# Gated keys transposed by VectorE blocks and DMA instead of TensorE, weights in pieces of 768, first step's layout by products

## Chip, cores and metric

The kernel runs on one core of one Trainium2 chip. The metric is the device time of one execution in microseconds (us), as the median of several runs. On one core a run counts as fast unless it is over 1.5% above the fastest of the same kernel; only fast runs are compared. One run of each kernel is profiled; all views below are of such profiled runs. In them PE is TensorE and PEld its loading of weights, DVE is VectorE, ACT ScalarE, POOL GpSimd and SP SyncE; L486 is line 486 of that kernel's program. PEclk is the clock granted to TensorE, as a share of full speed; in a row of digits each stands for one fortieth of the span, in tenths (9 is 90% or more).

## The reference, cut to what matters

```python
# attention: q, k, v, f_logit are (4, 8, 768, 48)
f = 1.0 / (1.0 + np.exp(-f_logit))
for t in range(S):
    state = f[:, :, t, :, None] * state + np.einsum('bhd,bhe->bhde', k[:, :, t], v[:, :, t])
    y[:, :, t] = np.einsum('bhd,bhde->bhe', q[:, :, t], state)
# bridge: x is (3072, 384); w_in (384, 2048), w_out (2048, 384)
x = y.transpose(0, 2, 1, 3).reshape(B * S, H * D)
h = x @ w_in
g = np.maximum(h, 0.0) + alpha * np.minimum(h, 0.0)
return g @ w_out
```

## The kernel before

The recurrence is computed in chunks of 128 tokens of two batches: 12 **steps** (2 pairs of batches, 6 chunks each). A step has four stages. `prepare` (VectorE and ScalarE) makes products of the gates; `carry` (TensorE) makes `off` (a product of gated queries and keys), transposes the gated keys (`pk`, copied to `ksn`) and computes the update of the state (`pd`, added into `vs`); `attend` makes `raw`, `qu` (masked into `ad`, copied to `A`) and the output `py`, which is copied to `y` and laid out by DMA as `xT`; `network` makes 8 groups of `ph` (each with `neg` on ScalarE and `g` on VectorE) and then 64 `po`. The results of TensorE go to tiles in a memory called PSUM, which the program takes in turn from two pools of banks, as below. In the traces a product that takes a bank again starts after the bank's last reader has ended: `pd` of the kernel before at 80.20 us, 0.10 us after an `ad` (78.25 + 1.85).

```python
psa = ctx.enter_context(tc.tile_pool(name="psa", bufs=2, space=bass.MemoryType.PSUM))
psn = ctx.enter_context(tc.tile_pool(name="psn", bufs=4, space=bass.MemoryType.PSUM))
def pair(name):     # off, pk, pd, raw, qu, py: two pairs of PSUM banks in turn
    return psa.tile([128, 2, 512], F32, tag="pair", name=name)
def bank(name):     # ph, po: four banks in turn
    return psn.tile([128, 512], F32, tag="net", name=name)
# ... in carry:
        pk = pair(f"pk_{i}")
        for u in range(U):
            for hp in range(HP):
                a = (u * HP + hp) * NC2
                nc.tensor.transpose(pk[:, u, hp * 128:(hp + 1) * 128], ks[:, a:a + 2].rearrange("p c s t -> p (c s t)"), ident)
        ksn = work.tile([128, U, HP * 128], F32, tag="ksn", name=f"ksn_{i}", bufs=1)
        for u in range(U):
            nc.scalar.copy(ksn[:, u], pk[:, u])
        yield
        pd = pair(f"pd_{i}")
        # ... 64 small products of ksn and vs
# ... in network:
        for f in range(0, NF, 2):
            ph = bank(f"ph{f}_{i}")
            # ... products of w_in_sb and xT
            nc.scalar.activation(neg, phv, AF.Relu, scale=-1.0)
            for j in range(2):
                nc.vector.scalar_tensor_tensor(g[:, j], neg[:, j], om[:, f + j:f + j + 1], phv[:, j],
                                               ALU.mult, ALU.add)
            yield
        po = [bank(f"po{u}_{i}") for u in range(U)]
        # ... 64 products of g and w_out_sb
```

The weights arrive as 64-bit numbers in pieces of 512 columns. ScalarE makes `pos` and `neg` of a piece, VectorE makes `lead`, `power` and the low part, and an accumulating DMA adds `lead` to it. The instruction order of TensorE, VectorE and ScalarE is set by hand, in strings of letters. `P` is the next part of this step's `prepare`, `Q` the same of the following step, `O` of `carry`, `S` of `attend`, `n` the next group of the previous step's `network`; `a` and `w` are the two halves of a w_in piece, `b` and `v` of a w_out piece; a digit repeats. Each of the three engines is given its instructions in exactly this order.

```python
    first = (
        "P2 a2 P2 w a2 w P O w P a w S2 O w Q S2 a w a S a S Q w2",
        "a P w a w a P w n P a n w b v w S b v n b n O v b v n b v S P S n b O b v n b S v2 n2 S n b v Q b v b n v b v2 Q3 S n Q",
        # ... two more
    )
    usual = "O n2 S n2 S2 n O n Q n Q n S n2 S Q n S Q2 n Q"
```

## Time and profile before

| | before |
|---|---|
| time, median of 3 runs | 657.95 us (657.88 to 659.75) |
| span of the profiled run | 658.4 us |
| TensorE busy | 93% |
| end of step 0 (its last `po`) | 109.97 us |
| a steady step, `off` to `off` | 50.34 us |
| from 10 to 110 us: VectorE busy, DMA share | 92%, 90% |

In a timeline a row has the start, the time from the first to the last of the merged instructions, engine, line, operation, output and inputs; the square bracket says how long the engine sat idle just before, and what ended that. The prediction below shows the main views of the kernel before. Its times for 512, 768 and 1024 elements (684, 954 and 1218 ns) are those of VectorE's TENSOR_TENSOR on fp32 there (`us`, `qd` and `k`).

### The profile page before, as it was taken

To read this page: it belongs to the slowest core of one execution; us is meant where nothing else is said; L and a number is where in the kernel's file an instruction comes from. 1 tells how busy PE (TensorE), PEld (TensorE's weight loads), DVE (VectorE), ACT (ScalarE), POOL (GpSimd) and SP (SyncE) were. 2 spreads that over 40 slices of the span, in tenths; PEclk is the share of its full clock that TensorE was granted. 3 is DMA by queue.
4 is the path that set the end of the run, shared out by engine and by line. 5 is a ranking of instruction groups with operands and counts; after the bars stand their busy time and mean duration, and the time that the engine had idled before them with its cause. 6 is when DMAs were issued, how large, how long until landed. Compare 5 with 4: busy or idle time off the path is not lost.

```text
span 658.4 us, 17032 instructions
## 1 busy us (share of the span) xinstructions
PE 615.5 (93%) x7392; PEld 458.0 (70%) x7392; DVE 420.2 (64%) x897; ACT 267.0 (41%) x493; POOL 69.9 (11%) x109
## 2 busy tenths in 40 slices
PE   0548899999999999999999999999999999999997
PEld 0436766866876876876876876876876786786874
DVE  5999889693863685685585586486387486360220
ACT  5855882543443242451451550550460451431210
POOL 8222332000010000000000001001001000000000
PEclk9857999999999999999999999999999999999999
DMA  6979986122212122112013113023023011001000
GB/s 225 302 207 269 282 233 159 35 65 73 66 37 68 35 52 87 33 40 86 28 53 81 31 62 81 26 66 80 26 66 81 26 34 25 26 2 25 24 1 24
DMA packets 29129, 53.03 MB, mean 81 GB/s; under 512 B 4320, under 2 KB 16864, under 8 KB 29056
## 3 DMA queue, kind: packets, MB, share of 16 engines
q0 software_dynamic: 9616, 27.92, 15.4%
q1 hardware_dynamic: 13584, 21.63, 10.6%
q10 hardware_dynamic: 5856, 2.40, 1.7%
q8 instruction: 58, 0.95, 0.6%
q14 instruction: 15, 0.12, 0.1%
HBM read 36.21 MB, written 4.72 MB: 62 GB/s over the span
## 4 chain that ended last, share of the span: by engine, by line
PE 84%; issue 7%; POOL 4%; DVE 2%; ACT 1%; DMA 1%; POOLq 0%
PE po L502 36%; PE ph L486 35%; PE py L456 3%; PE qu L431 3%; PE raw L416 3%; PE pk L369 2%; PE pd L381 2%; POOL w_in_sb L191 1%; PE off L356 1%; POOL w_out_sb L191 1%; DMA w_out_sb<-w_out_lead 1%; DVE us L289 0%; POOL vs L138 0%; ACT A L340 0%; POOL vs L247 0%
## 5 line engine op out<-in xcount | busy, mean ns | idle before, releaser
L486 PE MATMUL ph<-xT,w_in_sb 128*128 128x256 f32 x1152 | 264.3, 387 | 10.3 <-DMA xT<-y 10.3
L502 PE MATMUL po<-w_out_sb,g 128*128 128x384 f32 x768 | 253.0, 488 | 0.3 <-DMA w_out_sb<-w_out_lead 0.3
L486 PEld LDWEIGHTS ph<-xT,w_in_sb 128*128 128x128 f32 x1152 | 218.1, 192 | 44.7 <-DMA w_in_sb<-w_in_lead 11.3
L502 PEld LDWEIGHTS po<-w_out_sb,g 128*128 128x128 f32 x768 | 144.9, 190 | 97.7 <-DMA w_out_sb<-w_out_lead 0.9
L494 DVE SCALAR_TENSOR_TENSOR g<-neg,om,ph 128x256 f32<-128x256 f32 x192 | 83.1, 476 | 152.0 <-ACT neg L491 151.9
L491 ACT ACTIVATE neg<-ph 128x512 f32<-128x512 f32 x96 | 57.7, 601 | 152.8 <-PE ph L486 124.8
L508 ACT COPY o<-po 128x384 f32<-128x384 f32 x24 | 11.5, 478 | 115.2 <-PE po L502 115.2
L436 DVE COPY_PREDICATED ad<-mquad,qu 128x224 f32<-128x224 int32 (+6 forms) x168 | 50.3, 300 | 8.5 <-DVE ad L422 0.5
L465 ACT COPY y<-py 128x512 f32<-128x512 f32 x24 | 12.9, 591 | 81.2 <-PE py L456 81.2
L289 DVE TENSOR_TENSOR us<-us,fs 128x768 f32<-128x768 f32 (+2 forms) x72 | 44.5, 618 | 0.3
L422 DVE COPY_PREDICATED ad<-mraw,raw 128x256 f32<-128x256 int32 (+1 forms) x96 | 42.3, 441 | 2.7
L445 ACT COPY A<-ad 32x256 f32<-32x256 f32 x96 | 38.4, 400 | 3.8 <-DVE ad L436 2.5
L391 DVE TENSOR_TENSOR vs<-vs,f 48x768 f32<-48x768 f32 x20 | 19.1, 953 | 30.4 <-PE py L456 30.0
L275 ACT COPY us<-qd 128x256 f32<-128x256 f32 x48 | 29.6, 666 | 12.2 <-DVE qd L258 7.4
L258 DVE TENSOR_TENSOR qd<-qd,f 128x768 f32<-128x768 f32 (+2 forms) x36 | 27.1, 752 | 8.2 <-ACT qd L253 8.2
L340 ACT COPY A<-q 48x512 f32<-48x512 f32 x48 | 29.6, 617 | 6.3 <-DMA xT<-y 5.5
L237 POOL DMA_DIRECT2D k<-in_kT x11 | 8.4, 761 | 222.6 <-PE raw L416 197.6
L456 PEld LDWEIGHTS py<-A,vs 128*64 128x64 f32 x768 | 25.1, 145 | 7.2 <-issue 6.2
L431 PE MATMUL qu<-us,k 48*32 48x112 f32 x1536 | 26.4, 265 | 2.6 <-DVE us L289 1.7
L456 PE MATMUL py<-A,vs 128*64 128x64 f32 x768 | 26.9, 231 | 0.9 <-DVE vs L397 0.8
L356 PE MATMUL off<-q,kh 48*32 48x32 f32 x768 | 9.4, 199 | 18.3 <-DVE q L307 18.3
L416 PEld LDWEIGHTS raw<-qd,k 48*32 48x32 f32 x1536 | 18.1, 108 | 10.6 <-issue 10.2
(64 smaller groups left out, 451.1 us busy)
## 6 DMA issues: line engine op xcount, KB each, us to landing
w_in_raw<-in_w_in SPq DMA_DIRECT2D x12, 511.8 KB, 5.9
w_out_raw<-in_w_out SPq DMA_DIRECT2D x12, 511.8 KB, 5.8
f<-in_fT POOLq DMA_DIRECT2D x11, 512.0 KB, 4.1
q<-in_qT POOLq DMA_DIRECT2D x11, 512.0 KB, 4.1
k<-in_kT POOLq DMA_DIRECT2D x11, 512.0 KB, 4.3
out<-o SPq DMA_DIRECT2D x24, 192.0 KB, 1.9
vs<-in_v POOLq DMA_DIRECT2D x22, 192.0 KB, 3.5
w_in_sb<-w_in_lead POOLq DMA_DIRECT2D x12, 256.0 KB, 6.1
```

The costliest lines, as they stand in the source:

```text
L275: nc.scalar.copy(q4[:, :, :, r], qdv[r][:, :, :, 0])
L289: nc.vector.tensor_tensor(us[:, :, UO[m]:UO[m] + 4 * n].rearrange("p g (i r) -> p g i r", r=4), us[:, :, skip:skip + 4 * n].rearrange("p g ...
L416: nc.tensor.matmul(raw[DB * j:DB * (j + 1), par, hp * C:hp * C + QW], lhsT=k[r_, g * DB:(g + 1) * DB], rhs=qd[r_, g], start=True, stop=True)
L422: nc.vector.copy_predicated(adu[:, :, :, d:4], mraw[:, d, :, d:4].bitcast(I32).unsqueeze(1).broadcast_to((128, H, NB, n)), rv[:, :, QO[d]: ...
L431: nc.tensor.matmul(qu[DB * j:DB * (j + 1), par, hp * UW + 4:(hp + 1) * UW], lhsT=k4[r_, g * DB:(g + 1) * DB], rhs=us[r_, g, 4:UW], start=T ...
L436: nc.vector.copy_predicated(ad[:, u, :, :, 4 * m:DB], mquad[:, lo:lo + n].bitcast(I32).unsqueeze(1).unsqueeze(1).broadcast_to((128, 2, HP, ...
L445: nc.scalar.copy(A[s_, u, :, s_], ad[s_, u].rearrange("p r h t -> p (r h) t"))
L456: nc.tensor.matmul(py[64 * par:64 * par + 64, u, o:o + CH], lhsT=vs[bp][:, cc, u, hd * D:hd * D + 64], rhs=A[:, u, par * HP + hp, CH * cc: ...
L486: nc.tensor.matmul(ph[:, j * T:(j + 1) * T], lhsT=w_in_sb[:, kt, (f + j) * 128:(f + j + 1) * 128], rhs=xT[:, kt], start=(kt == 0), stop=(k ...
L491: nc.scalar.activation(neg, phv, AF.Relu, scale=-1.0)
L494: nc.vector.scalar_tensor_tensor(g[:, j], neg[:, j], om[:, f + j:f + j + 1], phv[:, j], ALU.mult, ALU.add)
L502: nc.tensor.matmul(po[u][:, 0:DM], lhsT=gs[f // 2][:, f % 2, u * C:(u + 1) * C], rhs=w_out_sb[:, f], start=(f == 0), stop=(f == NF - 1))
```

## The change

The intent is to take the transposes off TensorE, which is busy nearly all the time, and to shorten the start: fewer and larger weight pieces, and a first layout that needs no DMA. What VectorE's transpose leaves in `kt` is put in place in `ksn` by 16 DMAs a step, 32 rows of `kt` in each. The instruction orders are rewritten as well, that of the start and the usual one. The diff, cut to its core:

```diff
-WP = 512
-RAWS, TOPS, POWERS, LEADS = 5, 3, 2, 4
+WP = 768
+AT_ONCE = 1
+RAWS, TOPS, POWERS, LEADS = 4, 3, 1, 3
 ...  prepare: the two first steps do half of the q work and of its A copies
+        some = slice(0, GC) if c else slice(1, GC, 2)
-        for cc in range(NC2):
+        for cc in range(0 if c else 1, NC2):
 ...  prepare, last part
+        if c:
+            kt = work.tile([128, 2 * WP], F32, tag="raw", name=f"kt_{i}", bufs=RAWS)
+            nc.vector.transpose(kt[:, 0:W], ks.rearrange("p g s t -> p (g s t)"))
+            ksn = x["ksn"] = work.tile([128, U, HP * 128], F32, tag="ksn", name=f"ksn_{i}", bufs=1)
+            for a in range(4):
+                n = min(32, D - 32 * (a % 2))
+                for b in range(NJ):
+                    nc.sync.dma_start(out=ksn[32 * b:32 * (b + 1)]...[:, :, 32 * a:32 * a + n],
+                                      in_=kt[32 * a:32 * (a + 1), 0:W]...[:, :, b, 0:n])
 ...  carry: pk, its transposes and the ksn copies only "if not c"
-                        nc.tensor.matmul(pd[64 * par:64 * par + 64, cc, o:o + D],
-                                         lhsT=ksn[s_, u, hp * 128 + 64 * par:hp * 128 + 64 * par + 64],
+                        nc.tensor.matmul(pd[rows(par), cc, o:o + D],
+                                         lhsT=ksn[s_, u, hp * 128 + 64 * par:hp * 128 + 64 * par + D],
-                    nc.vector.tensor_copy(then[:, :, par:H:2], now)
+                    nc.scalar.copy(then[:, :, par:H:2], now)
 ...  attend, first step: xT by products with a shifted identity
+        if not (bp or c):
+            for kt in range(NK):
+                b = bank(f"xt{kt}_{i}")
+                for hp in pairs:
+                    nc.tensor.matmul(b[:, 0:T], lhsT=dense[:, o:o + 128], rhs=y[:, :, hp], ...)
+                nc.scalar.copy(xT[:, kt], b[:, 0:T])
 ...  order (all four strings of `first` are new; the second is shown)
-        "a P w a w a P w n P a n w b v w S b v n b n O v b v n b v S P S n b O b v n b S v2 n2 S n b v Q b v b n v b v2 Q3 S n Q",
+        "w P2 a w b n w n S v b v n b n v n O n b v n P b S2 v n b S v Q b n O n v Q S b v2 S n Q3 n Q",
-    usual = "O n2 S n2 S2 n O n Q n Q n S n2 S Q n S Q2 n Q"
+    usual = "O n S n2 S Q n S Q S O Q n2 Q n3 S Q S n3 Q"
```

## The prediction

> **What bounds the kernel now.** I read the page first (busy shares, clock row), then the chain of waits in order of time, then busy time by stretch, then who waited for whom.
>
> ```profile
> PE 615.5 (93%) x7392; PEld 458.0 (70%) x7392; DVE 420.2 (64%) x897; ACT 267.0 (41%) x493; POOL 69.9 (11%) x109
> ...
> PEclk9857999999999999999999999999999999999999
> ```
>
> TensorE is busy for 93% of the span. The clock row is below 9 only in slices 2 to 4, so the two halves of the run differ: a start of about 110 us and a steady part. One steady step in the chain, from one `off` to the next:
>
> ```profile
> 261.15 0.69 PE off L356 x50
> 261.83 1.02 PE pk L369 x8
> 262.86 5.18 PE ph L486 x24
> 268.04 0.85 PE raw L416 x60
> 268.89 0.85 PE qu L431 x61
> 269.73 5.38 PE ph L486 x24
> 275.11 0.85 PE raw L416 x60
> 275.96 0.84 PE qu L431 x61
> 276.80 2.79 PE ph L486 x12
> 279.59 1.08 PE pd L381 x64
> 280.66 7.97 PE ph L486 x36
> 288.63 10.32 PE po L502 x32
> 298.95 2.02 PE py L456 x64
> 300.97 10.52 PE po L502 x32
> 311.49 0.69 PE off L356 x50
> ```
>
> Every piece is TensorE and begins where the last ends: 311.49 - 261.15 = 50.34 us a step, no wait. Here only TensorE work taken out shortens the run. Also visible: 24 `ph` take 5.18 after `pk` but 5.38 after `qu`, and 32 `po` take 10.32 after `ph` but 10.52 after `py`. Passing from small tiles to full ones costs 0.2.
>
> The start, by stretch (us, then busy time of PE, PEld, DVE, ACT, POOL with counts, clock, DMA share, GB/s):
>
> ```profile
> 30.00:40.00 10.00, 8.09 (x192) 7.12 (x192) 9.09 (x23) 7.75 (x16) 2.64 (x4) 0.50 0.63 184
> 40.00:50.00 10.00, 1.50 (x4) 1.09 (x4) 9.26 (x18) 5.28 (x10) 3.75 (x6) 0.50 0.89 219
> 50.00:60.00 10.00, 7.63 (x86) 5.68 (x84) 9.98 (x21) 5.22 (x9) 3.25 (x4) 0.73 1.01 302
> ```
>
> TensorE has half clock and almost nothing to do at 40 to 50; VectorE is nearly full throughout, DMA full in places. What TensorE waited for:
>
> ```profile
> PE off L356 <- DVE q L307: 18.3, 1, 18.3
> ...
> PE ph L486 <- DMA xT<-y: 10.3, 2, 8.8
> ```
>
> The first is the first preparation on VectorE. The second is the first step's layout transfer: its ten DMAs go out from 41.6 and 42.2, when the weight loads already fill the DMA engines, and `ph` starts only at 48.5. From 102.13, where the last wait (for a piece of w_out) ends, TensorE never waits again except in the tail. So the time is: the moment step 0's last `po` is done (110.0 in the timeline), plus 548.4 us of dense work.
>
> [...]Trace: 512 elements 684[...], 768 954[...], 1024 1218[...], and I use it for the transpose. [...]Trace: eight `pk` start at 312.10 and `ph` at 313.03, 116 ns each[...]. [...]The 48 KB layout transfer took 4.6 us to land in the first 110 us and 3.2 in the steady part[...]
>
> **The change, part by part.**
>
> 1. `pk` leaves TensorE in the ten steps with c > 0 (80 of 96 transposes). From 312.10 to 313.03 is 0.93 us; `off` to `ph` will now pay the passage to full tiles itself, in the timeline 0.15 (`qu` from 319.00 takes 64 x 13.2 ns = 0.85, `ph` starts at 320.00). Net 0.78 x 10 = 7.8 us, all on the path. Two ScalarE copies of 0.59 a step go too; ScalarE is 39% busy, worth nothing.
>
> 2. In its place VectorE gets one transpose of 1024 elements, about 1.2 us (estimate as above), at 67% busy in the steady part: hidden. SP gets 16 DMAs a step. The layout DMAs take about 0.6 us each to issue, so some 10 us, plus 3 to land. They start when the source is ready and the layout transfer of the same step has released the buffer (`y` and `ksn` share one): in before about 7.5 us after `py`. So landed about 21 us after `py`. The instruction order has `pd` 14.5 us after the next `off`, and that 15.7 us after `py`: 30 us. Some 9 us of slack: hidden.
>
> 3. `pd` loads 48 columns of weights instead of 64. 64 `pd` take 1.08 us, 16.9 ns each[...]; if weight loads set that pace, up to a quarter (0.27 us a step, 2.7 in ten) goes. I take half: 1.3 us.
>
> 4. Weight pieces of 768: 16 instead of 24. In before a piece costs 0.34 + 0.60 + 0.20 = 1.14 us of VectorE from start to start; 768 adds 0.13 + 0.27 + 0.07, so 1.61. 24 x 1.14 = 27.4 against 25.8. One add on VectorE (+0.87) takes the place of one accumulating DMA; two pairs of `vs` copies go to ScalarE (-2.1); the halved `q` work of the two first steps gives -1.1; two scans (+1.3) are now ahead of the last piece. Net 2.6 us less until the last piece of w_out, 98.4 instead of 101. More comes from the order, since VectorE loses 7 us to waits between 10 and 101.
>
> 5. The first layout by products: 6 products, 12 passes of 216 ns = 2.6 us at full clock, 5 at the half clock, in time that TensorE has idle, and three copies. `y` now comes later, about 44 us: `A`'s second half is behind a weight piece and the `us` copies on ScalarE. So `ph` starts at about 50, but then without the second wait of 1.5 us, with all three tiles ready[...]. Ten DMAs leave the congested stretch, and SP no longer holds the raw weight loads behind them.
>
> I then walked the start with these durations in the instruction order. VectorE has the second step's `us` at 55.5 (before 60.7); the first two `ph` groups and `raw`, `qu` are done at 58.2 (before 61.9). TensorE then has 41.8 us of work up to the last piece of w_out (six `ph` groups 15.5, second attention 8.2, 56 `po` 18.1), so about 101 at best. The last piece leaves VectorE at 92 to 94 and lands 8 us later, 384 KB instead of 256, some 6.0 us before. Total DMA work until then was 95 of 110 us (the queues' shares over that stretch, summed), about 5 of it goes (layout, one accumulate), and DMA was 90% busy from 10 to 110; that also gives 100 to 102. With 2.6 us of `po` behind it step 0 ends at 103.7 to 105.5, I take 105: 5 us less.
>
> Sum: 7.8 + 1.3 + 5.0 = 14.1; 657.95 - 14.1 = 643.8.
>
> **Rivals.** (a) Late `ksn`: 4096 runs of 128 or 64 bytes a step might cost more than I count. SP would have to take 1.2 us an issue to use up the slack; then every step gains a wait at `pd`, and the time is 650 or more. For it: no transfer in the trace has such short runs. Against: the slack. (b) The start gains nothing, because VectorE and DMA are full there anyway and the larger pieces land later: only 7.8 to 9 us, time 649. For it: DMA share 1.01 in places. Against: less work on both. (c) The start gains as much as the order allows: step 0 ends at 102, `pd` pays in full: 639.5.
>
> **Range and chances.** The steady part gives 7.5 to 10.5, the start 1 to 8: 639.5 to 648.5. A gain over 2% needs 13.2 us, just under my 14.1, so it is hardly better than even: 0.58 faster, 0.41 within, 0.01 slower.
>
> **What would show it.** Chain: ten steady steps of about 49.4 instead of 50.34, with `off` straight to `ph`, the latter with +0.2. `pd` below 1.08 for 64. No wait of TensorE for a `ksn` DMA. A transpose of about 1.2 us. Step 0's last `po` at 105, `ph` from about 50, no wait for `xT` there. Wrong if `pd` waits for `ksn`, if w_out lands later than 103, or if SP's long queue delays the layout transfer and `ph` waits for `xT` in the steady part.

## The result

The changed kernel took 674.84 us (median of 4 runs, 674.09 to 675.73), the kernel before 658.28 on the same chip. The ratio is 1.0248, 95% interval 1.0226 to 1.027: **slower by 2.5%**, where 643.8 had been predicted. Here and below a ratio is formed from the fast runs of both kernels; it is not quite the ratio of the medians.

The page of the changed kernel: busy shares, the clock row, the engines' shares of the chain that ended last.

```profile
PE 617.6 (92%) x7324; PEld 451.5 (67%) x7324; DVE 427.6 (64%) x880; ACT 253.8 (38%) x460; POOL 66.3 (10%) x103
...
PEclk9999899999999999999989999989999999999999
...
PE 65%; DVE 19%; DMA 6%; issue 4%; ACT 2%; POOL 2%; ACTq 0%; DVEq 0%; POOLq 0%; SPq 0%
```

TensorE executes 68 instructions fewer and yet is busy for longer, VectorE has entered the chain with 19%, and the clock row has an 8 in two slices of the steady part. By stretch, from the two chains of waits:

| stretch | before | after | difference |
|---|---|---|---|
| to the end of step 0 | 109.97 | 109.95 | 0.0 |
| from there to the `off` that ends the first steps | 100.85 | 99.67 | -1.2 |
| seven usual steps | 352.53 | 368.34 | +15.8 |
| the rest | 95.05 | 94.34 | -0.7 |

So two things have to be explained: the usual steps, which were to be 0.9 us shorter, are 2.3 us longer on average (15.8 / 7), and the start gained nothing. A usual step of the changed kernel, TensorE's timeline:

```profile
261.39 0.76 PE L385 MATMUL off<-q,kh 48*32 48x32 f32 x64
262.08 2.86 PE L529 MATMUL ph<-xT,w_in_sb 128*128 128x256 f32 x12
...
276.58 0.94 PE L412 MATMUL pd<-vs,ksn 64*48 64x48 f32 x64
277.45 10.63 PE L529 MATMUL ph<-xT,w_in_sb 128*128 128x256 f32 x48
290.07 5.54 PE L545 MATMUL po<-w_out_sb,g 128*128 128x384 f32 x16 [2.00 <-DVE g L537]
```

`off` goes straight to `ph`, `pd` is short, nothing waits for `ksn`. But the last four `ph` groups end at 288.07, and `po` starts 2.00 us later, released by a `g`. VectorE's timeline of the same time shows where that `g` was:

```profile
281.52 0.85 DVE L537 SCALAR_TENSOR_TENSOR g<-neg,om,ph 128x256 f32<-128x256 f32 x2
...
283.71 0.95 DVE L422 TENSOR_TENSOR vs<-vs,f 48x768 f32<-48x768 f32 x1
284.76 1.12 DVE L426 TENSOR_TENSOR vs<-vs,pd 48x384 f32<-48x384 f32 x2
285.80 1.21 DVE L293 TENSOR_TENSOR us<-us,f 128x1024 f32<-128x1024 f32 x1
286.94 1.21 DVE L308 TENSOR_TENSOR k<-k,kr 128x1024 f32<-128x1024 f32 x1
288.07 0.94 DVE L302 TENSOR_TENSOR us<-us,fs 128x768 f32<-128x768 f32 x1
289.05 1.65 DVE L537 SCALAR_TENSOR_TENSOR g<-neg,om,ph 128x256 f32<-128x256 f32 x4
```

There is no gap: between the two rows of `g` stand 6.7 us of other work. `po` takes two of the four `net` banks, and those are free only when `g` has read the `ph` group in them: the second of these `g` ended at 289.92 (289.05 + 0.87), and `po` began at 290.07. In the kernel before the `g` of the second of the two groups began at 284.17 and took 0.87, while `po` began at 288.63; there were 3.6 us to spare:

```profile
284.17 0.87 DVE L494 SCALAR_TENSOR_TENSOR g<-neg,om,ph 128x256 f32<-128x256 f32 x2 [0.30 <-ACT neg L491]
```

The waits of the changed kernel, in total, with times and the longest:

```profile
ACT neg L534 <- DVE g L537: 43.2, 16, 5.2
...
PE po L545 <- DVE g L537: 14.3, 7, 2.3
```

Seven waits, one in each of the seven usual steps. They sum to 14.3 of the 15.8 us, though these steps also save about 1 us each. The clock adds to it. Four of the seven steps take 51.85 us, three take 53.5 to 53.8. In the longer ones the wait at the same place is followed by a stretch at half clock: `po` x16 takes 7.23 us from 341.91, against 5.54 from 290.07. By stretch (columns as in the prediction):

```profile
288.00:290.00 2.00, 0.07 (x1) 0.00 (x0) 1.97 (x5) 0.00 (x0) 0.04 (x1) 1.00 0.62 104
...
343.00:345.00 2.00, 2.00 (x4) 1.02 (x4) 2.00 (x4) 0.26 (x1) 0.00 (x0) 0.50 0.03 8
```

In the first row TensorE is idle and VectorE full, at clock 1.00; in the second the granted clock is 0.50, just after the same wait one step later. In windows of 0.1 us each of the three stretches at half clock is 3.41 us long, which is where the 1.7 us come from; the point on the clock below has their times.

In the start, `ph` began at 52.79 us (predicted about 50), the first `raw` and `qu` of the second step were done at 59.74 (predicted 58.2), TensorE lost 4.4 us to waits after that (2.92 of them inside one `qu`, put down to "issue"), and step 0 ended at 109.95 instead of 105.

### The profile page after: what moved, and what is told of

It reads as the page before. It is cut to its first block, busy times and chain, and to the rows that moved or that the text cites. A ratio compares the mean times of both kernels' runs of the same rounds, so it can differ in the third digit from the quotient of the medians.

```text
span 672.3 us, 17083 instructions
## 1 busy us (share of the span) xinstructions
PE 617.6 (92%) x7324; PEld 451.5 (67%) x7324; DVE 427.6 (64%) x880; ACT 253.8 (38%) x460; POOL 66.3 (10%) x103
## 4 chain that ended last, share of the span: by engine, by line
PE 65%; DVE 19%; DMA 6%; issue 4%; ACT 2%; POOL 2%; ACTq 0%; DVEq 0%; POOLq 0%; SPq 0%
PE po L545 36%; PE ph L529 21%; PE py L487 3%; DVE g L537 3%; DMA w_in_raw<-in_w_in 2%; DVE ad L467 2%; DVE qd L271 2%; PE qu L462 2%; DVE ad L453 2%; DMA w_in_sb<-w_in_lead 2%; PE raw L447 2%; DVE k L308 1%; DVE us L293 1%; DVE us L302 1%; DVE vs L426 1%
## 5 line engine op out<-in xcount | busy, mean ns | idle before, releaser
L545 PE MATMUL po<-w_out_sb,g 128*128 128x384 f32 x768 | 259.8, 497 | 15.1 <-DVE g L537 14.3
L487 PE MATMUL py<-A,vs 128*64 128x64 f32 x768 | 27.4, 232 | 4.4 <-ACT A L476 3.1
L462 PE MATMUL qu<-us,k 48*32 48x112 f32 x1536 | 28.2, 273 | 2.9 <-issue 2.9
L358 ACT COPY A<-q 48x512 f32<-48x512 f32 x44 | 27.1, 617 | 2.6 <-DVE q L324 2.0
L447 PE MATMUL raw<-qd,k 48*32 48x80 f32 x1536 | 23.3, 243 | 3.2 <-issue 2.5
```

The lines of the kernel that those rows point to most:

```text
L447: nc.tensor.matmul(raw[DB * j:DB * (j + 1), par, hp * C:hp * C + QW], lhsT=k[r_, g * DB:(g + 1) * DB], rhs=qd[r_, g], start=True, stop=True)
L462: nc.tensor.matmul(qu[DB * j:DB * (j + 1), par, hp * UW + 4:(hp + 1) * UW], lhsT=k4[r_, g * DB:(g + 1) * DB], rhs=us[r_, g, 4:UW], start=T ...
L487: nc.tensor.matmul(py[64 * par:64 * par + 64, u, o:o + CH], lhsT=vs[bp][:, cc, u, hd * D:hd * D + 64], rhs=A[:, u, par * HP + hp, CH * cc: ...
L545: nc.tensor.matmul(po[u][:, 0:DM], lhsT=gs[f // 2][:, f % 2, u * C:(u + 1) * C], rhs=w_out_sb[:, f], start=(f == 0), stop=(f == NF - 1))
```

## The experiments

All 18 kernels were correct, and all their runs were fast except one of `b1_new_usual`, which is left out of its ratio. The times are medians, the ratios to the kernel before on the same chip. The kernel before took 658.3 to 660.1 us on these chips, so between chips the ratios are compared rather than the times, and a time that was expected may come out 1 to 2 us higher for that reason alone. A difference counts from 2% on: only the changed kernel, `b1_new_usual` and `a3_pe_transposes` are slower by that rule, and all others count as the same as the kernel before, though their intervals lie below 1. "Step" is from one `off` to the next in the steady part.

### The steady part: the order, or the transposes?

**Theory: the new usual order** puts the third `Q` (3.3 us of VectorE) ahead of the `g` that `po` needs. **Rival: the transposes** and their DMAs load VectorE and SP.

`a1_prep_after_g`: the changed kernel with one letter moved.

```diff
-    usual = "O n S n2 S Q n S Q S O Q n2 Q n3 S Q S n3 Q"
+    usual = "O n S n2 S Q n S Q S O n2 Q2 n3 S Q S n3 Q"
```

> One move in the steady order of the changed kernel: the third part of the preparation goes behind the two network groups that now come after it. Order theory: in a steady step po waits for the PSUM banks of the fifth and sixth ph group, whose g stand on VectorE behind that third part (3.3 us); the wait (2.0 to 2.4 us a step, and 1.7 more in the steps where the clock then drops) vanishes, seven steps fall from 51.85/53.5 to 49.4 to 49.8, total 648 to 652. Transposes theory (the 1.25 us on VectorE and the 16 small DMAs delay the step): no change, about 672.

Measured: 653.08 us, ratio 0.9896 (0.9876 to 0.9917), a step of 49.47 us. Moving one letter is worth 21.8 us (674.84 - 653.08), or 3.5% by the ratios, which allow for the two chips (some 23 us). It also settles the account of the seven steps: at 49.47 they would take 346.3 us, so 22.0 of the 368.34 are excess; 14.3 of it are the waits, 5.1 the half clock (three times 7.23 - 5.54), and 2.6 were not followed up. The lines of its TensorE timeline that answer to those above, and then that of VectorE's `g`:

```profile
276.12 10.63 PE L529 MATMUL ph<-xT,w_in_sb 128*128 128x256 f32 x48
286.59 5.32 PE L545 MATMUL po<-w_out_sb,g 128*128 128x384 f32 x16
```

```profile
284.62 1.66 DVE L537 SCALAR_TENSOR_TENSOR g<-neg,om,ph 128x256 f32<-128x256 f32 x4
```

The `g` comes right after `vs` and ahead of `us` and `k`, and `po` follows `ph` without a wait.

`a2_old_usual`: the changed kernel with the usual order of before.

```diff
-    usual = "O n S n2 S Q n S Q S O Q n2 Q n3 S Q S n3 Q"
+    usual = "O n2 S n2 S2 n O n Q n Q n S n2 S Q n S Q2 n Q"
```

> The changed kernel with the steady order of the kernel before. Order theory: steps of 49.3 us without a wait at po, total 647 to 651. Transposes theory: about 672, as the transposes and their DMAs are all still there.

Measured: 653.99 us, ratio 0.9899, a step of 49.3 us. The transposes are in it, and they cost nothing that shows.

`b1_new_usual`: the converse, the kernel before with only the new usual order.

```diff
-    usual = "O n2 S n2 S2 n O n Q n Q n S n2 S Q n S Q2 n Q"
+    usual = "O n S n2 S Q n S Q S O Q n2 Q n3 S Q S n3 Q"
```

> The kernel before with only the steady order of the changed kernel; TensorE still transposes. Order theory: the wait at po appears without any transpose on VectorE: 2.0 to 4 us in each of seven to eight steps, total 674 to 686. Transposes theory: stays at 658.

Measured: 678.11 us, ratio 1.0272 (1.0249 to 1.0294), without a single transpose on VectorE. Its profiled run fell in the slow state, so only the presence of the wait is read from it, not its size:

```profile
PE po L502 <- DVE g L494: 12.4, 7, 1.8
```

Again seven waits of `po` for `g`. The order alone makes the kernel slower by as much as the whole change did.

`a3_pe_transposes`: the changed kernel with `pk` on TensorE in every step.

```diff
-        if c:
+        if False:
             kt = work.tile(...)
-        if not c:
+        if True:
             pk = pair(f"pk_{i}")
```

> The changed kernel, order and all, but with the TensorE transposes in every step and no VectorE transpose and no small DMA. Order theory: the wait at po stays and TensorE has 0.8 to 1.0 us more a step: 680 to 684. Transposes theory: the loss goes, 655 to 662.

Measured: 691.6 us, ratio 1.0479, a step of about 54.6 us; slower than either theory had it. The transposes theory, under which the loss would have gone, is out. The seven usual steps take 381.1 us against 368.3 in the changed kernel. The one at full clock takes 52.96 (51.85 there); the other six have the stretch at half clock, against three there, which is some 5 us of the 12.8. `qu` also waits for the `ksn` copies, but only 0.18 us a step.

### The parts of the change by themselves

`b2_dve_transposes`: the kernel before with the VectorE transposes, their DMAs and the narrower `pd`, in the old usual order.

```diff
+        if c:
+            kt = ...; nc.vector.transpose(...); 16 DMAs to ksn      # as in the change
-        pk = pair(f"pk_{i}")                                         # now only "if not c"
-        ... 64 columns of pd weights
+        ... 48 columns
-   first[1] "... Q3 S n Q",   first[2] "... n P S n S Q n Q"
+   first[1] "... Q3 S n Q2",  first[2] "... n S n S Q n Q"
```

> The kernel before, its start and its steady order, with only the VectorE transposes and small DMAs for c > 0 (and pd at 48 columns, which comes with them). Prediction's steps 1 to 3: ten steps of 49.3 instead of 50.34 us and nothing else: 648 to 649.5. If the new start of the changed kernel gains 5 us as the prediction said, this must be 5 us slower than the changed kernel with the old steady order; if the new start gains nothing or loses, it is equal or faster by 2 to 5 us.

Measured: 651.75 us, ratio 0.9886 (0.9857 to 0.9915), a step of 49.33 us. It is no slower than `a2_old_usual` (0.9899), so the new start gains nothing.

`b3_pd48`: the kernel before with only the narrower `pd`.

```diff
-                        nc.tensor.matmul(pd[64 * par:64 * par + 64, cc, o:o + D],
-                                         lhsT=ksn[s_, u, hp * 128 + 64 * par:hp * 128 + 64 * par + 64],
+                        nc.tensor.matmul(pd[rows(par), cc, o:o + D],
+                                         lhsT=ksn[s_, u, hp * 128 + 64 * par:hp * 128 + 64 * par + D],
```

> The kernel before with only pd at 48 instead of 64 weight columns. Prediction's step 3, as the profiles now show it (64 pd in 0.86 instead of 1.08 us): 0.22 x 11 to 12, so 2.4 us less, 655.5 to 656. Rival (the 0.22 came with the new order or the DMA'd operand): no change, 658.

Measured: 657.89 us, ratio 0.9975 (0.9964 to 0.9986), a step of 50.12, so the rival is out. `pd` takes 0.86 instead of 1.08 us, so this part is worth 0.22 us a step, and `pk` the other 0.79 (50.34 - 49.33 - 0.22).

The cost of issuing the DMAs on SP and of the transpose on VectorE, from the view of the tile `kt` of the changed kernel (min, median and max in ns, then first and last start):

```profile
L368 SPq DMA_DIRECT2D ksn<-kt x160: 585/609/1792, 114.7 to 578.7; - x160
L363 DVE STREAM_TRANSPOSE kt<-ks x10: 1245/1245/1246, 113.4 to 561.6; 128x1024 f32<-128x1024 f32 x10
```

### The start: do products, lead buffers or VectorE's load set its end?

`a5_dma_layout`: the changed kernel with the usual order of before and with the first layout by DMA.

```diff
-        if not (bp or c):
+        if False:
             for kt in range(NK):     # the products
```

> The changed kernel with the old steady order and the first layout again by ten DMAs. Prediction's step 5 (products save the waits for xT and free SP): 2 to 4 us slower than with the products, 653 to 657. Rival (the start is held by the accumulating DMAs and VectorE, not by xT): within 1 us of it, 650 to 654.

Measured: 652.3 us, ratio 0.9893 (0.988 to 0.9905), as `a2_old_usual`. `ph` starts only at 55.45 us and waits again until 58.64, and still step 0 ends at 111.3. An earlier `ph` is worth nothing there.

`a7_dma_layout_leads4`: the same with four lead buffers (and without the tile `dense`, which is not used then), since VectorE waited 1.3, 0.5 and 2.6 us for them in the changed kernel.

```diff
-RAWS, TOPS, POWERS, LEADS = 4, 3, 1, 3
+RAWS, TOPS, POWERS, LEADS = 4, 3, 1, 4
```

> The changed kernel with the steady order of before, the first layout by DMA (so the mask tile is not needed) and four lead buffers instead of three; otherwise the version that ran at 652.3 us, ratio 0.9893. Theory A, VectorE's waits for lead buffers (1.3 + 0.5 + 2.6 us in the changed kernel's trace) hold back the last piece of w_out and with it the end of step 0: step 0's last po ends 2 to 4 us earlier, total 648.5 to 650.5, ratio 0.983 to 0.9865. Rival B, those waits lie beside the landing of the pieces, which DMA paces: the same as with three, 651 to 653.5, ratio 0.987 to 0.991.

Measured: 653.35 us, ratio 0.9912 (0.9897 to 0.9926). The rival holds: a fourth buffer gains nothing.

`c1_transposes_products`: `b2_dve_transposes` with the first layout by products, pieces of 512.

```diff
+    dense = const.tile([128, 6 * D], F32, tag="dense", name="dense")     # as in the change
+        if not (bp or c):
+            for kt in range(NK): ...                                     # the products, as in the change
```

> The kernel before with the VectorE transposes and with the first layout by products, in its own start order with pieces of 512. If the products are worth what the prediction says, 2 to 4 us less than without them: 645 to 647. If the weight path holds the start: the same 648 to 649.5.

Measured: 650.0 us, ratio 0.9859 (0.9843 to 0.9876). The interval overlaps that of `b2_dve_transposes`, so a gain by the products is not shown. Here `ph` starts at 45.89, after which the second step's `qu` waits 8.69 us for VectorE's `us`, until 61.02.

Three changes to `c1_transposes_products` were meant to use that. `c2_more_groups_first` fills the wait with two more `ph` groups, `c3_less_vector_work` takes 3.2 us off VectorE (half of the q work and of its `A` copies in the two first steps, `vs` copies to ScalarE), `c4_both` has both.

```diff
 c2
-        "a P w a w a P w n P a n w b v w S b v n b n O v b v ...
+        "a P w a w a P w n P a n w b v w n n S b v b O v b v ...
 c3
+        some = slice(0, GC) if c else slice(1, GC, 2)      # as in the change
-                    nc.vector.tensor_copy(then[:, :, par:H:2], now)
+                    nc.scalar.copy(then[:, :, par:H:2], now)
```

> The kernel before with VectorE transposes and the first layout by products, pieces of 512, with two ph groups moved ahead of raw and qu of the second step (in the version without that move, 650.0 us and ratio 0.9859, qu waits 8.69 us for us copies from VectorE while ph groups stand behind it). Theory A, TensorE's own work after that wait sets the end of step 0: 2 to 5 us less, 645 to 648. Rival B, the landing of the last pieces of w_out sets it, since VectorE finishes the last piece at 100 us either way: step 0 still ends at 109 to 110, total 649 to 651, ratio 0.984 to 0.988.

> As the version with VectorE transposes and products (650.0, ratio 0.9859), and in addition the two first steps do half of the q work and the vs copies go to ScalarE: about 3.2 us less on VectorE ahead of the last piece of w_out. Theory A, VectorE's queue up to that piece (100.0 us) sets the end of step 0: last piece at 97 to 98, step 0 ends 2 to 3 us earlier, total 646.5 to 648, ratio 0.980 to 0.983. Rival B, DMA sets it (90% busy from 10 to 110 us): the last piece leaves VectorE earlier, but lands as late, total 649 to 651.

> Both the less VectorE work and the two ph groups moved ahead. If VectorE's queue bounds the start and TensorE's order follows: 643.5 to 647.5, ratio 0.975 to 0.982, the best so far. If DMA bounds it: 649 to 651, as the others.

Measured: 653.11 (0.9912), 653.87 (0.9915) and 656.8 us (0.9961). All three missed, upwards. In `c2` the wait moved to `off`, which needed a pair of banks that VectorE's `ad` had not read yet (7.12 us). In none of the three does TensorE wait for a w_out piece, so neither VectorE's last piece nor its landing sets the end here. In all three the end of step 0 follows the second step's attention. What made `c3` worse had to be in one of its halves.

`d1_half_queries` has only the half of the q work, `d2_state_copies` only the moved `vs` copies.

```diff
 d1
+        some = slice(0, GC) if c else slice(1, GC, 2)
-        for cc in range(NC2):
+        for cc in range(0 if c else 1, NC2):
 d2
-                    nc.vector.tensor_copy(then[:, :, par:H:2], now)
+                    nc.scalar.copy(then[:, :, par:H:2], now)
```

> The best version (650.0 us, ratio 0.9859) with the two first steps doing half of the q work and half of the A copies, the vs copies left on VectorE: 1.4 us less on VectorE, of which 0.7 ahead of the second step's us chain. Theory (the end of step 0 is the end of the second step's first qu plus 46 us): qu ends at about 62.0 instead of 62.7, step 0 ends 0.7 earlier, total 649 to 650. Rival (the vs copies on ScalarE were not what made the run with both worse): about 653, as that run.

> The best version (650.0 us, ratio 0.9859) with only the vs copies of the two first steps moved from VectorE to ScalarE. Theory, in ScalarE's order they stand ahead of the A copies and wait for pd: y comes at 45 instead of 40.6, qu of the second step ends at about 67, step 0 ends at 113 to 114, total 653.5 to 655, ratio 0.990 to 0.993. Rival, 2.1 us less on VectorE is a gain as the prediction had it: 648 to 649.5.

Measured: 649.29 us, ratio **0.9834** (0.9813 to 0.9854), the fastest of all, though its interval overlaps that of `c1_transposes_products`, and 655.99 us, ratio 0.9936 (0.9921 to 0.995). Both theories hold: `qu` ends at 62.0 and 67.4 and step 0 at 108.3 and 113.7. The two halves also add up to `c3_less_vector_work`: 0.9859 - 0.0025 + 0.0077 = 0.9911, with 0.9915 measured. ScalarE in `d2_state_copies`:

```profile
34.30 0.96 ACT L413 COPY vs<-pd 48x384 f32<-48x384 f32 x2 [5.70 <-PE pd L397]
...
37.74 3.34 ACT L461 COPY A<-ad 32x256 f32<-32x256 f32 x8
...
45.10 1.07 ACT L481 COPY y<-py 128x512 f32<-128x512 f32 x2
```

The copies that took 2.1 us of VectorE now make ScalarE wait 5.70 us for `pd`, and all that stands behind them comes late: `y` at 45.10, against 40.61 in `c1_transposes_products`.

`d3_state_on_vector`: does that hold for the changed kernel too? It is `a1_prep_after_g` with these copies back on VectorE.

```diff
-                    nc.scalar.copy(then[:, :, par:H:2], now)
+                    nc.vector.tensor_copy(then[:, :, par:H:2], now)
```

> The changed kernel with the mended steady order (653.08 us, ratio 0.9896) and the vs copies back on VectorE. There the vs copies follow the first A copies on ScalarE and only 0.96 us of them is ahead of y. Theory (qu plus 46 us): y up to 1 us earlier, VectorE 1.05 us more before the second step's us: within 1 us of 653.1, ratio 0.988 to 0.991. Rival, they are the cause there as well: 649 to 651.

Measured: 652.65 us, ratio 0.9889, against 0.9896: no difference. In the changed kernel's own order the copies stand behind the first `A` copies. On VectorE they come late as well: `py` waits 5.84 us for them in `d3_state_on_vector`.

`d4_us_first`: `d1_half_queries` with the second step's `us` chain put first on VectorE.

```diff
+        us_first = bp and not c
+        if us_first:                       # us 3 to 7 at once, then the products of k and q
+            for m in range(3, NB):
+                earlier(m)
-        "a P w a w a P w n P a n w b v w S b v n b n O v b v n b v S P S ...
+        "a P a P w2 a n n S a w P w b n w b v n O b v b v n b v2 S P S ...
```

> As the run with half of the q work, and in the second step VectorE does the us chain ahead of k, q products and of two weight pieces, so that TensorE's qu comes earlier; the w_in pieces moved behind are not needed before 72. Theory (qu plus 46 us, until w_out binds): qu ends at 57 to 58 instead of 62.7, the second step's off at about 65 instead of 70.1, step 0 ends at 104.5 to 106.5 and TensorE may wait a little for the last w_out piece; total 645 to 648, ratio 0.978 to 0.983. Rival (weights through VectorE and DMA bound the start): TensorE waits for w_in and w_out pieces instead, step 0 ends at 109 to 110 again, total 649.5 to 651.

Measured: 656.84 us, ratio 0.9951, a miss. `qu` ended at 55.3 and `off` began at 61.2, even earlier than expected; then `pk` waited 3.99 us for `ks` and `pd` waited 8.45. The `pd` wait in the kernel before, where it is already there, and in `d4_us_first`, each with what VectorE did then:

```profile
80.20 1.15 PE L381 MATMUL pd<-vs,ksn 64*64 64x48 f32 x64 [2.18 <-issue]
```

```profile
78.25 1.85 DVE L422 COPY_PREDICATED ad<-mraw,raw 128x256 f32<-128x256 int32 x4
```

```profile
84.50 1.53 PE L412 MATMUL pd<-vs,ksn 64*48 64x48 f32 x64 [8.45 <-issue]
```

```profile
82.55 1.85 DVE L453 COPY_PREDICATED ad<-mraw,raw 128x256 f32<-128x256 int32 x4
```

The first two rows are of the kernel before, the last two of `d4_us_first`. The profile puts both waits down to "issue", that is to nothing it sees. But `pd` starts 0.10 us after `ad` has read `raw` out of the pair of banks that `pd` takes next (78.25 + 1.85 = 80.10, and 82.55 + 1.85 = 84.40). In `d4_us_first` that `ad` stood behind a w_out piece for which VectorE waited 4.04 us.

`e1_us_first_ad_first` and `e2_ad_first` test this: `d4_us_first` and `d1_half_queries` with that `S` ahead of the last `v`.

```diff
 e1
-        "... n b v2 S P S n b O ...
+        "... n b S v2 P S n b O ...
 e2
-        "... v n b v S P S n b O ...
+        "... v n b S v P S n b O ...
```

> As the run with the us chain first (656.84 us, ratio 0.9951), with VectorE's ad copies of the second half of the second step ahead of two w_out pieces instead of behind them. Theory (pd waits for its pair of PSUM banks, which ad frees): pd starts at 76 to 77 instead of 84.5, step 0 ends at 105.5 to 109, total 645.5 to 649.5, ratio 0.978 to 0.984. Rival (the 8 us are TensorE's own, as a fetch of instructions under DMA load): pd again at 84 or so, total 655 to 657.

> As the run with half of the q work (649.29 us, ratio 0.9834), with the ad copies of the second half of the second step ahead of one w_out piece. Theory: pd's wait of 1.15 us goes (pd at 77.5 instead of 78.6); step 0 ends up to 1 us earlier, if the last w_out piece (wait of 0.37 there) does not take it: 648 to 649.5, ratio 0.9815 to 0.984. Rival (fetch): pd waits as long, total 649 to 650.

Measured: 652.23 us (0.9894, 0.9878 to 0.9909) and 650.09 us (0.9861, 0.9838 to 0.9885). `pd` of `e1`:

```profile
77.89 0.94 PE L412 MATMUL pd<-vs,ksn 64*48 64x48 f32 x64 [0.27 <-PE ph L528]
```

VectorE ahead of it:

```profile
75.92 1.87 DVE L453 COPY_PREDICATED ad<-mraw,raw 128x256 f32<-128x256 int32 x4
```

The wait fell from 8.45 to 0.27 us in `e1`, and in `e2` `pd` follows `ph` at 80.40 without one. In `e1` `pd` still starts 0.10 us after this `ad` (75.92 + 1.87 = 77.79), as it does in `d1_half_queries` (78.50 and 78.60): it moved with the reader, so the banks were its cause. The time still did not fall as expected. In `e1` TensorE now waits three times later on: 0.94 us for a `g`, and 1.18 and 2.58 for pieces of w_out, whose VectorE work had been put behind; step 0 ends at 112.37. In `e2` the second step's `qu` came 1.25 us later than in `d1_half_queries`, and with it the end.

The starts of these kernels side by side, in their profiled runs:

| kernel | `qu` of the second step ends | step 0 ends | waits of TensorE in between |
|---|---|---|---|
| before | 61.9 | 109.97 | 2.18 `pd`, 0.5 others |
| after | 59.7 | 109.95 | 2.92 inside `qu`, 0.80 w_out, 0.7 others |
| c1_transposes_products | 62.7 | 109.30 | 0.9 |
| c2_more_groups_first | 62.1 | 111.68 | 7.12 `off`, 1.32 `pk`, 0.7 |
| c3_less_vector_work | 67.4 | 113.57 | 1.1 |
| c4_both | 68.1 | 116.74 | 5.90 `off`, 1.32 `pk`, 0.7 |
| d1_half_queries | 62.0 | 108.31 | 1.15 `pd`, 0.37 w_out |
| d2_state_copies | 67.4 | 113.70 | 0.7, 0.42 w_out |
| d4_us_first | 55.3 | 116.31 | 8.45 `pd`, 3.99 `pk`, 0.5 |
| e1_us_first_ad_first | 56.3 | 112.37 | 2.94 `pk`, 0.94 `g`, 3.76 w_out, 0.3 |
| e2_ad_first | 63.3 | 109.40 | 0.4 |

Where nothing waits much, the end is `qu` plus 46 to 47 us of dense TensorE work. Where `qu` is brought forward, waits for VectorE come up in its place, for its `ad`, `ks`, `g` or a weight piece. Between 10 and 110 us VectorE is busy for 91 to 93% of the time before, after and in `d1_half_queries`. The runs fit a start bounded by VectorE, with attention and weights competing for it; they do not prove that no order could do better. Nor do they separate VectorE from DMA, which is busy for 90 to 92% of the same time and for which VectorE and TensorE wait in places: no run takes load off DMA alone.

## Why the prediction was wrong, point by point

- **The overlap in the usual steps.** This is the step that failed. Parts 1 and 3 book 9.1 us as gain "all on the path", which takes it that TensorE goes on without a wait in every steady step ("ten steady steps of about 49.4"). For VectorE the prediction relied on "at 67% busy in the steady part: hidden". That holds for the transpose itself, but a share of busy time does not say whether what a later instruction needs comes in time. The new `usual` string was used to work out when `pd` comes, and that was the only slack that was checked; what it puts between two `g` was not. It put 6.7 us of other work there, and `po` needs the banks that the second of them frees. So `po` waited some 2.0 us in each of seven steps (14.3 in all), three stretches at half clock added 5.1, and the steps took 51.85 to 53.8 us instead of 49.4. The order cost 21.8 us (`a1_prep_after_g` against the changed kernel), and 18.1 us on the kernel before without any other change. In the trace VectorE takes its work in the order of the string: it had the two `ph` groups' `g` at 289.05 only after `us`, `k` and `us`, which run from 285.80 to 289.01. The rivals named a wait for `ksn` and a start without gain; none named a wait for a bank.
- **Parts 1 and 3, the steady gain**: right, once the order is. 49.43 us a step follows from the predicted sizes (0.78 and 0.13 off 50.34), 49.33 and 49.47 were measured. `pk` is worth 0.79. The share taken for `pd` was too small: 0.22, not 0.13; all but 0.05 of the quarter goes. The prediction has 116 ns from one `pk` to the next; the records of the `pk` weight loads are 140 ns long (median, kernel before). Nothing in the forecast rests on the 116. That weight loads set the pace of `pd` was the assumption; the records of these loads fell from 135 to 122 ns (median) with the change, and no run separates them from the products.
- **Part 2, transposes and their DMAs**: sizes right (1.245 us for 128x1024, where the estimate was about 1.2 from the 1218 ns of a TENSOR_TENSOR of that size; 0.609 us an issue; 10.4 us of SP a step; 2.0 us from issue to landing, median, for 16 KB and for 32), no `ksn` wait in the changed kernel, and the work is hidden (`a2_old_usual`, `b2_dve_transposes`). Rival (a) is out.
- **Parts 4 and 5, the start**: "5 us less" failed. Rival (b) had the right outcome for the start, but its reason is not what the trace shows: a w_out piece of 384 KB took 6.1 us to land (median), one of 256 KB 6.0, where the walk had 8. The saving on VectorE was mis-sized: a piece of 768 takes 1.73 us of it from start to start (86.38 to 88.11), not 1.61 (of the additions, 0.13 + 0.27 + 0.07 as the estimate, the first and the last came out, at 0.13 and 0.08; the middle one was 0.38), so 16 pieces cost 27.7 us, as much as the 24 of before (27.4). The last w_out piece was to leave VectorE at 92 to 94 and began its last VectorE step at 100.18. TensorE was 1.5 us later at the second step's `qu` and then lost 4.4 us to waits, where the walk had allowed for none but the last piece. The `vs` copies were counted as 2.1 us gained; alone, `d2_state_copies` shows them as a loss of some 5 us (ratio 0.9936 against 0.9859). The products brought `ph` forward, but `a5_dma_layout` without them is as fast.
- **The clock**: the prediction reckons with it in the start alone, where it was higher than before (0.98 from 10 to 110 us, 0.85 before). The products of the first layout took 5.37 us (47.58 to 52.95) at a granted 1.00, where part 5 has 2.6 at full clock. In three of seven usual steps a wait of 2.0 to 2.3 us was also followed by a stretch at 0.50, which cost 1.7 us there (`po` x16 7.23 against 5.54). In windows of 0.1 us these stretches begin at 342.86, 448.68 and 554.49, each 3.41 us long and 105.81 us after the one before; `po` had gone on 0.95, 1.07 and 1.45 us earlier. The other four waits are as long, 2.00 to 2.04 us, and the clock stayed at 1.00 after them. What sets the three apart is not shown; no run tests it.
- **The sum.** Had the order been harmless, the result would have been 653.08 us (`a1_prep_after_g`; 651 if its ratio is taken on 657.95): above the predicted range too, which ends at 648.5, since the start gave nothing. The best version, `d1_half_queries`, keeps the pieces of 512, the old usual order, the transposes, the products and half of the q work: 649.29 us, ratio 0.9834. It beats both kernels, by 1.7% over the one before; its whole interval stays short of 2%.
- **Open**: the wait of 2.5 to 3.2 us inside one `qu` of the start, always after 39 of its 64 products, in the changed kernel, `a1`, `a2`, `a3` and `d3`. It falls into a time when DMA is full (share 1.05 from 77.09 to 80.01 in the changed kernel); an instruction fetch is only a guess. One packet of the queue that the profile calls `q8 instruction` does fall into that wait in all five (from 77.5 us in the changed kernel, where the wait runs from 77.09 to 80.01), but no run tests it. `raw` in the first step waits 0.3 to 2.5 us in the same way in most kernels.

## What to carry to other kernels

When an order of instructions is rewritten, follow the engine whose order changed from one buffer release that the critical engine needs to the next, and sum the work that now stands between; the busy share does not show it. A wait that the profile names "issue" may be a wait for a PSUM bank, as those of 2.18 and 8.45 us before `pd` here: look for the reader that ended just before it (0.10 us here). Work moved to an idle engine is only free if the place in its order doesn't make what follows wait for its input (5.70 us in `d2_state_copies`).
